# Talking-heads attention and squared-ReLU FFN on one core: when v and w_in are loaded in the first batch, and where dummy matmuls may stand

## The chip, the core and the metric

The kernel runs on one core of a Trainium2 chip. The metric is the device time of the whole program in microseconds (us). TensorE is called PE, VectorE DVE, ScalarE ACT, GpSimd POOL and SyncE SP, as in the profile.

## What is computed

The reference, cut to what matters (B = 8 batches, H = 12 heads, S = 448 tokens, D = 64; the FFN has 768 x 2048 and 2048 x 768 weights):

```python
scores = q @ k.T / 8                           # per batch and head
scores = einsum('bhij,hg->bgij', scores, w_pre)   # mix heads
attn   = softmax(scores)                          # over keys j
attn   = einsum('bhij,hg->bgij', attn, w_post)    # mix heads again
x      = (attn @ v)  -> (B*S, H*D) = (3584, 768)
out    = relu(x @ w_in)**2 @ w_out
```

## The kernel before, in words

**The stages of a batch.** q and k are transposed on PE (`t_qk`, L522; the last 64 tokens of q by `t_tail`, L550) and evacuated by DVE or ACT (L426, L428). `score` (L660) multiplies q and k for 128 query rows at a time, a row block `r` of which there are 3 and one of 64 rows (r = 0); the scores of all heads land, heads in the free dimension, in an `snat` tile. Mixing heads on PE needs the heads in the partition dimension, so SP issues DMAs within the on-chip memory that lay 10 tokens x 12 heads on 120 partitions (`relayout`, `move`, L689). There are 45 such chunks to a batch. In the first two row blocks of batch 0, three chunks share one larger move of 315 KB (a "triple") into five buffers, which are borrowed from tiles that are free then (`osb0`, `osb1`, and three in an `h2` tile, which the trace shows as `h`). In batch 0 the 18 triple chunks are mixed by three matmuls each (L780), all others by one (L784).

**A chunk** (`chunk`) is: mixing on PE (L780 or L784), maximum on DVE (L789), exp with its sum on ACT (L792), reciprocal on DVE (L798), the weights `wq` on POOL (L801), the second mixing on PE (L808), and its evacuation into `atb` by DVE or ACT. There are six sets of `es`, `mn`, `sm`, `rc`, `wq` (NE = 6): chunk n cannot be mixed before the second mixing of chunk n - 6 is through.

**After chunks.** `av` (L848) multiplies with v, ACT puts the result into `xt`, and FFN units follow as columns of tokens are complete: 96 matmuls with w_in (L901) per unit and row group, ReLU on ACT, square on POOL (L917), then matmuls with w_out (L933), evacuation and store.

**What sets the order.** Nothing is issued in the order in which it is written. Each operation is put into a `Planner` with an engine, an assumed duration in ns, a priority (chunk number plus an offset) and what it depends on; `run` goes through an assumed time and always takes the ready operation of the lowest priority on each engine. What comes out is one fixed order for each engine; on the chip every engine works through its list in that order and waits by semaphores. Score and relayout priorities contain the constant `AHEAD` (relayout: chunk number - AHEAD). Transfers are modelled as rows times ns, `alone` or `shared` with the other queue. Where PE has nothing ready, `run` may put in a dummy matmul on a zero tile (`still`, L1144), under the condition that the planner's model of PE's clock is slow or the share of busy time lately is under 0.55.

**Loads in the first batch.** POOL issues all loads: three of k, two of the q tails, three of q, ahead of everything else. `first_batch` then adds a POOL copy `hold` (L1067) that reads the `snat` tile of the r = 0 scores after it is complete; the two halves of v (336 KB each, `vs`) and after them the six tiles of w_in (512 KB each, `w1`, L1019) wait for this copy (`opened`). w_out follows in four loads that are gated by the `wq` of chunks 18, 21, 24, 27 (`gate`), and the q and k of batch 1 by those of chunks 13 and 16.

The dummy rule and the priority of a relayout read:

```python
if item is None and eng == "PE" and free and IDLE_FROM <= t < IDLE_END and (
    clock.at(t) > 1 or clock.share(t - SPELL, t) < IDLE_LOW
):
...
pri = n - AHEAD
```

Of the kernel before, what the change touches and what calls it, by code (L numbers as in the profile page):

```python
# [10 lines left out]
BF16 = mybir.dt.bfloat16  # L11
F32 = mybir.dt.float32

B, H, S, D = 8, 12, 448, 64
DMODEL = H * D
DFF = 2048
NPAIR = H // 2
# [22 lines left out]
PIECE = NPAIR // 2  # L40
NE = 6
NSCH = 11
AHEAD = 7.4
FIFO = 50
IDLE_NS, IDLE_COLS, IDLE_FROM, IDLE_END, IDLE_LOW = 112, 256, 1300, 130000, 0.55
SPELL, PHASE, DROP, RISE = 3413, 1700, 0.4, 0.8
# [29 lines left out]
TRI_IN = (0, 1)  # L76
W2_AT = [18, 21, 24, 27]
Q1_AT = [13, 16]
LAST_W1 = 4
TAIL0, Q0 = 19, 0.7  # L80
EARLY0 = 0

# [35 lines left out]
class Planner:  # L118
# [8 lines left out]
    def add(self, eng, ns, pri, fn, deps=(), lat=60, bank=None, frees=None, mode=0):  # L127
        op = Op(eng if isinstance(eng, dict) else {eng: ns}, lat, pri, fn, list(deps), bank, frees, mode)
        self.ops.append(op)
        return op  # L130
# [6 lines left out]
    def run(self):  # L137
        order, events, n = [], [], 0
# [21 lines left out]
        t, mode, clock = 0, 0, Clock()  # L160
# [16 lines left out]
        while True:  # L177
            for eng, heap in ready.items():
                if eng in queues:
                    x = queues[eng]  # L180
# [49 lines left out]
                        kept.remove(first)  # L230
                        item, op, args = first, first[2], []
                if item is None and eng == "PE" and free and IDLE_FROM <= t < IDLE_END and (
                    clock.at(t) > 1 or clock.share(t - SPELL, t) < IDLE_LOW
                ):
                    op = Op({"PE": 0}, 0, 0, self.still, [], None, None, mode)
                    op.eng, op.ns, op.at = "PE", IDLE_NS * clock.at(t), t
                    clock.spells.append((t, t + op.ns))
                    order.append((op, [free[0], mode]))
                    busy[eng] = t + op.ns
                    heapq.heappush(events, (t + op.ns, n, None))  # L240
                    n += 1
# [22 lines left out]
            t = events[0][0]  # L264
            while events and events[0][0] == t:
# [3 lines left out]
                if isinstance(op, tuple) and isinstance(op[0], Queue):  # L269
                    x, turn_ = op  # L270
# [29 lines left out]
def kernel(  # L300
# [11 lines left out]
    nc = tc.nc  # L312
    P = nc.NUM_PARTITIONS

    sb = ctx.enter_context(tc.tile_pool(name="sb", bufs=1))
# [9 lines left out]
    vs = sb.tile([P_KEYS, H, NB, D], BF16, name="vs")  # L325
# [32 lines left out]
    def load_kv(dst, src, b, h0, h1):  # L358
        nc.gpsimd.dma_start(
            out=dst[:, h0:h1, :, :].rearrange("p h r d -> p h (r d)"),  # L360
            in_=src[b, h0:h1].rearrange("h (p r) d -> p h (r d)", r=NB),
        )
# [5 lines left out]
    for what in LOADS0:  # L368
# [15 lines left out]
        out=smask[:, :], in_=ident[0:KC, 0:KC].rearrange("p (s h) -> p s h", s=CI), axis=AX.X, op=ALU.add,  # L384
    )
    wmix = many(3, "wmix", [KC, P], BF16)
    for t_ in wmix:
# [4 lines left out]
        out=nmask[:, :], in0=smask[:, :], scalar1=-SCALE, scalar2=1.0, op0=ALU.mult, op1=ALU.mult,  # L392
# [3 lines left out]
        out=perm[:, :].rearrange("k (s x p) -> k s x p", s=CI, x=2),  # L396
        in_=ident[0:KC, 0:KC].rearrange("k (s p x) -> k s x p", s=CI, x=2),
    )
    for t_ in wmix[1:]:
        nc.vector.tensor_tensor(  # L400
            out=t_[:, 0:KC].rearrange("p (s h) -> p s h", s=CI),
# [4 lines left out]
        out=wback[:, :, :], in0=wpost_rep[:, :].unsqueeze(2).to_broadcast([KC, H, CI]),  # L406
# [5 lines left out]
        out=keep_m[:, :], in_=ident[0:KC, 0:KC].rearrange("p (s m g) -> p m s g", s=CI, m=3), axis=AX.XY, op=ALU.add,  # L412
# [19 lines left out]
    add = pl.add  # L432
# [12 lines left out]
    def load(rows, each, pri, fn, deps):  # L445
        if len(loads) >= 7:
            deps = list(deps) + [loads[-7]]
        op = add("POOL", 750, pri, fn, deps, lat=850)
        done = pl.moved("LOAD", rows, each[0], each[1], 0, [op], 1500)
        loads.append(done)  # L450
        return done

    q_in, k_in, v_in = {}, {}, {}
# [43 lines left out]
    score_ops, scopy = {}, {}  # L497
# [45 lines left out]
    def t_tail(b, g):  # L543
        key = ("f" if b == 0 else "g", "z", b, g)
        old = [score_ops[b - 1, 0, p] for p in range(3 * g, 3 * g + 3)] if b > 0 else []

        def mms(slot):
            v_ = slot[:, :].bitcast(BF16)
            for i in range(3):
                nc.tensor.transpose(v_[:, i * P:(i + 1) * P], qt[:, 3 * g + i, :], ident[:, :])  # L550

        def put(eng):
            copy(
                eng, zt[:, 3 * g:3 * g + 3, :].rearrange("p a c -> p (a c)"),
                slots[key][:, :].bitcast(BF16)[:, 0:3 * P],
            )

        pri = b * NCHUNK - (19 if b > 0 else TAIL0) + 3 * g
        mm = add("PE", 200, pri, keep(key, mms), [tail_in[b]] + old, lat=200, bank=key)
        ev = add({"DVE": 360, "ACT": 440}, 0, pri, put, [mm], frees=key)  # L560
        got_tail.setdefault(b, []).append(mm)
        for p in range(3 * g, 3 * g + 3):
            ready_tail[b, p] = ev
# [63 lines left out]
    def flip(b, r):  # L627
        return 1 - r if b == 0 and r < 2 and EARLY == 0 else r
# [4 lines left out]
    def store_of(b, r):  # L633
        return snat[flip(b, r) % 2]
# [9 lines left out]
    def groups(b, r):  # L644
        size = GROUP if b >= GROUP_AT and r > 0 else 1
        return [range(p, p + size) for p in range(0, NPAIR, size)]

    def score(b, r, group):
# [13 lines left out]
        first = [0, EARLY, C0[2], C0[3]][r] if b == 0 else C0[r]  # L662
        pri = b * NCHUNK + first - AHEAD - 0.6 - (0.7 if r == 0 else 1.4) * (NPAIR - p)
        n = b * (NJ + 1) + r - 2
# [19 lines left out]
    def block_of(c):  # L684
        r = sum(c >= c0 for c0 in C0) - 1
        return r, c - C0[r]

    def move(n, pri, ns, deps, outs, srcs, lat):
        op = add("SP", ns, pri, lambda: nc.sync.dma_start(out=outs, in_=srcs), deps, lat=680)  # L689
        rows, alone, shared = (8, 160, 130) if ns == 800 else (12, 70, 38) if ns > 700 else (6, 70, 38)  # L690
        done = pl.moved("DMA", rows, alone, shared, 0, [op], 500)
        relay.setdefault(n, []).append(done)
        return done

    def relayout(b, c):
# [6 lines left out]
        deps = list(scopy[b, r]) + (list(scopy[b, r - 1]) if r == 1 and cc == 0 else [])  # L702
        pri = n - AHEAD
        if r == 2 and cc == 0:
# [279 lines left out]
    def gate(step):  # L984
        return [wq_op[step]] if step in wq_op else []
# [14 lines left out]
    started = add("POOL", int(1000 * at_) + 700, -100, lambda: None)  # L1000
# [17 lines left out]
    def load_w1(c2, pri, more=()):  # L1018
        w1_in.append(load(16, (152, 148), pri, lambda: nc.gpsimd.dma_start(  # L1019
            out=w1[c2][:, :], in_=moe_w_in[c2 * 128:(c2 + 1) * 128, 0:DFF], max_dma_last_dim=4096,  # L1020
        ), [started, *more]))
# [7 lines left out]
        done.next.append(w2_in[f4])  # L1029
        w2_in[f4].left += 1  # L1030

    def load_half(b, n, x, deps):
        h0 = x * H // 2
        v_in[b].append(load(42, (46, 58), n, lambda: load_kv(vs, v, b, h0, h0 + H // 2), deps))

    def load_v(b, n, deps):
        v_in[b] = [load(42, (46, 58), n, lambda h0=h0: load_kv(vs, v, b, h0, h0 + H // 2), deps) for h0 in (0, H // 2)]

# [14 lines left out]
    def first_batch():  # L1053
        for i in range(NPAIR):
            if i == 0:
                v_in[0] = []
                for x in range(0):
                    load_half(0, -30 + x, x, [started])
        for p in range(NPAIR):
            t_qk(0, p)  # L1060
        for g in range(2):
            t_tail(0, g)
        for r in (1, 0):
            for p in groups(0, r):
                score(0, r, p)
        hold = sb.tile([P, NPAIR], BF16, name="hold")
        opened = add("POOL", 150, -6, lambda: nc.gpsimd.tensor_copy(  # L1067
            out=hold[:, :], in_=store_of(0, 0)[:, 0:NPAIR, 0],
        ), scopy[0, 0])
        for x in range(0, 2):  # L1070
            load_half(0, -5 + 0.1 * x, x, [opened])
        for i in range(NPAIR):
            load_w1(i, -4 + 0.1 * i, [opened])
        for n, c in enumerate(ORDER0):
            if c in C0[2:]:
                for p in groups(0, block_of(c)[0]):
                    score(0, block_of(c)[0], p)
            relayout(0, c)
            chunk(0, c)
            if n in W2_AT:  # L1080
                load_w2(W2_AT.index(n), n)
            if n in Q1_AT:
                load_ahead(1, n, 6 * Q1_AT.index(n))
            if c == C0[1]:
                for g in range(3):
                    av(0, 0, g, 0, P_ROWS)
                unit(0, 0)
            if c == C0[2]:
                for g in range(3):
                    av(0, 0, g, P_ROWS, XA)  # L1090
            if c == C0[3]:
                for g in range(3):
                    av(0, 1, g, 0, P_ROWS)
                unit(0, 1)
        for g in range(3):
            av(0, 1, g, P_ROWS, XB)
        unit(0, 2)
# [87 lines left out]
```

## Time and profile before

| What | us |
|---|---|
| median of 3 runs (587.54, 588.30, 588.59) | 588.3 |
| the profiled execution: device time | 587.99 |
| the profiled execution: span of its instructions | 586.2 |
| PE busy in the span | 569.0 (97%) |
| DVE busy | 486.9 (83%) |
| ACT busy | 470.5 (80%) |
| POOL busy | 326.4 (56%) |

How to read it: the span runs from the first to the last instruction that the profiler recorded, so 1.8 us of the device time lie around it. PE's matmuls are pipelined and their ends are modelled, so "busy" is not the same as "at its peak"; the 51 dummies count as busy too. A wait is put down to the semaphore that came last. On ACT and DVE, which evacuate what PE makes and carry the softmax, idle time matters only while PE waits for them.

### The profile page before, as it was taken

How to read it: one execution, taken by the hardware profiler on the slowest of the kernel's cores; microseconds unless marked ns; L12 is line 12 of the kernel's file. 1: busy time of each engine (PE TensorE's matmuls, PEld its weight loads, DVE VectorE, ACT ScalarE, POOL GpSimd, SP SyncE). 2: the span in 40 equal slices, each digit the busy share in tenths (PEclk: the TensorE clock that was granted, in tenths of full speed). 3: DMA queues.
4: the chain of work that ended last, by engine and by line, in shares of the span. 5: the costliest groups of instructions: out<-in, count | busy, mean ns of one | idle time of the engine just before them, and what ended most of it. 6: DMA issues, size and time to landing. Idle time of an engine off the chain costs nothing.

```text
span 586.2 us, 17120 instructions
## 1 busy us (share of the span) xinstructions
PE 569.0 (97%) x5802; PEld 407.8 (70%) x5802; DVE 486.9 (83%) x1241; ACT 470.5 (80%) x1239; POOL 326.4 (56%) x600
## 2 busy tenths in 40 slices
PE   8798999999999999999999999999999999999996
PEld 5446866777668676767767776876767766868783
DVE  5698999998899999999898888989798898989201
ACT  4597998889888898988888878888889888788330
POOL 4537557546666538744865538744856633735340
PEclk9899999999999999999999999999999999999999
DMA  8999969964796449965797639954597547322021
GB/s 96 190 216 221 208 143 174 192 160 116 130 196 164 122 115 173 190 134 142 114 173 171 135 100 173 184 146 124 100 176 177 133 112 146 102 82 79 1 55 54
DMA packets 132086, 82.33 MB, mean 140 GB/s; under 512 B 59582, under 2 KB 126286, under 8 KB 131998
## 3 DMA queue, kind: packets, MB, share of 16 engines
q1 hardware_dynamic: 85214, 58.42, 41.1%
q0 software_dynamic: 46784, 22.81, 30.9%
q8 instruction: 45, 0.74, 0.6%
q14 instruction: 43, 0.35, 0.2%
HBM read 45.62 MB, written 11.01 MB: 97 GB/s over the span
## 4 chain that ended last, share of the span: by engine, by line
PE 85%; ACT 4%; DMA 3%; DVE 3%; POOL 2%; issue 2%; SPq 0%; DVEq 0%; POOLq 0%; ACTq 0%
PE bank L933 24%; PE bank L901 24%; PE bank L808 13%; PE bank L784 10%; PE bank L848 6%; PE bank L660 6%; ACT es L792 2%; DMA sch<-snat 1%; DVE mn L789 1%; DMA osb<-snat 1%; PE bank L780 1%; ACT snat L428 1%; ACT hr L914 1%; PE bank L522 1%; DMA qt<-in_q_dram 1%
## 5 line engine op out<-in xcount | busy, mean ns | idle before, releaser
L792 ACT ACTIVATE es<-bank,mn 120x448 bf16<-120x448 f32 x360 | 229.6, 644 | 39.2 <-DVE mn L789 34.1
L801 POOL TENSOR_SCALAR wq<-wback,rc 120x120 bf16<-120x120 f32 x360 | 130.6, 367 | 179.1 <-DVE rc L798 104.0
L789 DVE TENSOR_REDUCE mn<-bank 120x1 f32<-120x448 f32 x360 | 210.2, 612 | 7.7 <-PE bank L780 4.5
L933 PE MATMUL bank<-w,h 128*128 128x384 bf16 x896 | 174.3, 325 | 0.9 <-ACT es L792 0.5
L426 DVE CAST atb<-bank 112x480 bf16<-112x480 f32 (+3 forms) x227 | 142.5, 636 | 28.9 <-PE bank L808 26.2
L901 PE MATMUL bank<-xt,w 128*128 128x256 bf16 (+1 forms) x1632 | 164.5, 253 | 0.2
L901 PEld LDWEIGHTS <-w 128*128 128x128 bf16 x1632 | 135.7, 98 | 21.9 <-issue 2.3
L917 POOL TENSOR_TENSOR h<-hr 128x512 bf16<-128x512 f32 x112 | 116.3, 1039 | 54.2 <-ACT hr L914 51.9
L808 PEld LDWEIGHTS <-es 120*112 120x112 bf16 (+1 forms) x1440 | 116.7, 130 | 38.2 <-issue 7.6
L808 PE MATMUL bank<-wq,es 120*112 120x120 bf16 (+1 forms) x1440 | 129.1, 217 | 3.0 <-POOL wq L801 2.0
L933 PEld LDWEIGHTS <-h 128*128 128x128 bf16 x896 | 83.5, 97 | 54.9 <-issue 5.2
L784 PE MATMUL bank<-sch,wmix 120*128 120x448 bf16 x334 | 103.2, 353 | 0.3
L426 DVE CAST snat<-bank 128x448 bf16<-128x448 f32 x164 | 96.3, 614 | 4.8 <-PE bank L660 3.3
L428 ACT CAST atb<-bank 112x480 bf16<-112x480 f32 (+3 forms) x157 | 82.5, 541 | 16.3 <-PE bank L808 14.7
L914 ACT ACTIVATE hr<-bank 128x512 f32<-128x512 f32 x112 | 67.1, 599 | 30.9 <-PE bank L901 25.2
L428 ACT CAST snat<-bank 128x448 bf16<-128x448 f32 x172 | 84.9, 551 | 3.7 <-PE bank L660 2.9
L792 ACT ACTIVATION_READ_ACCUMULATOR es<-bank,mn 120x1 f32 x360 | 76.0, 211 | 0.0
L798 DVE RECIPROCAL rc<-sm 120x1 f32<-120x1 f32 x360 | 53.4, 155 | 14.2 <-ACT es L792 12.0
L948 DVE COPY osb<-bank 128x384 f32<-128x384 f32 x56 | 30.9, 551 | 31.6 <-PE bank L933 31.3
L660 PE MATMUL bank<-kt,qz 64*128 64x448 bf16 x288 | 42.5, 354 | 0.4 <-ACT atb L428 0.2
L784 PEld LDWEIGHTS <-wmix 120*128 120x128 bf16 x342 | 30.3, 98 | 16.6 <-issue 6.7
L848 PE MATMUL bank<-atb,vs 112*64 112x192 bf16 (+3 forms) x864 | 41.0, 250 | 0.4 <-ACT atb L428 0.4
(60 smaller groups left out, 261.8 us busy)
## 6 DMA issues: line engine op xcount, KB each, us to landing
sch<-snat SPq DMA_DIRECT2D x318, 105.0 KB
out_dram<-osb SPq DMA_DIRECT2D x23, 360.0 KB
vs<-in_v_dram POOLq DMA_DIRECT2D x16, 336.0 KB, 9.0
ks<-in_k_dram POOLq DMA_DIRECT2D x14, 336.0 KB, 9.9
qs<-in_q_dram POOLq DMA_DIRECT2D x14, 288.0 KB, 8.9
w<-in_moe_w_in_dram POOLq DMA_DIRECT2D x6, 512.0 KB, 20.9
w<-in_moe_w_out_dram POOLq DMA_DIRECT2D x4, 768.0 KB, 25.1
out_dram<-osb SPq DMA_DIRECT2D x8, 192.0 KB
```

The costliest lines, as they stand in the source:

```text
L426: nc.vector.tensor_copy(out=out_, in_=in_)
L428: nc.scalar.copy(out=out_, in_=in_)
L660: nc.tensor.matmul(slot[:, 0:S], lhsT=lhsT, rhs=kt[i][half, :, at_, :], start=True, stop=True)
L784: nc.tensor.matmul(slot[:, 0:S], lhsT=wm[0:rows, :], rhs=src[0:rows, :], start=True, stop=True,)
L789: nc.vector.tensor_reduce(out=mn[i][0:rows, :], in_=slots[mk][0:rows, 0:S], axis=AX.X, op=ALU.min)
L792: nc.scalar.activation(out=es[i][0:rows, 0:S], in_=slots[mk][0:rows, 0:S], func=ACT.Exp, scale=-1.0, bias=mn[i][0:rows, 0:1], accum_out=sm ...
L801: nc.gpsimd.tensor_scalar(out=wq[i][0:rows, :, 0:ns], in0=wback[0:rows, :, 0:ns], scalar1=rc[i][0:rows, 0:1], scalar2=1.0, op0=ALU.mult, o ...
L808: nc.tensor.matmul(slot[0:P_KEYS, jb * H * ns:(jb + 1) * H * ns], lhsT=es[i][0:rows, jb * P_KEYS:(jb + 1) * P_KEYS], rhs=wq[i][0:rows, :, ...
L848: nc.tensor.matmul(v_[64 * hh:64 * hh + 64, i, 0:x1 - x0], lhsT=vs[:, 2 * c2 + hh, jb, :], rhs=atb[half][:, jb, 2 * c2 + hh, x0:x1], start ...
L901: nc.tensor.matmul(slot[:, j * w:(j + 1) * w], lhsT=w1[c2][:, (f0 + j) * 128:(f0 + j + 1) * 128], rhs=xt[:, c2, a:z], start=(c2 == 0), sto ...
L917: nc.gpsimd.tensor_tensor(out=h2_[:, f0:f0 + nf, 0:w], in0=hr[gi % 2][:, :].rearrange("p (f c) -> p f c", f=nf), in1=hr[gi % 2][:, :].rear ...
L933: nc.tensor.matmul(slot[:, 0:384], lhsT=h2_[:, ft, mt * 128:(mt + 1) * 128], rhs=w2[:, ft, nt * 384:(nt + 1) * 384], start=(ft == 0), stop ...
```

## The change

v is loaded directly behind q, without the `hold` copy, which goes away. The six loads of w_in are gated by the `wq` of chunk 0 and have the priority 0. Three constants of the planner change: `AHEAD` 7.4 to 7.2, the assumed time per row of a triple move on an otherwise idle queue 160 to 205 ns, and a dummy is allowed in any PE gap of the planner's first 9000 ns.

```diff
-AHEAD = 7.4
+AHEAD = 7.2
...
-LAST_W1 = 4
+W1_AT = [0, 0, 0, 0, 0, 0]
...
                 if item is None and eng == "PE" and free and IDLE_FROM <= t < IDLE_END and (
-                    clock.at(t) > 1 or clock.share(t - SPELL, t) < IDLE_LOW
+                    t < 9000 or clock.at(t) > 1 or clock.share(t - SPELL, t) < IDLE_LOW
                 ):
...
-        rows, alone, shared = (8, 160, 130) if ns == 800 else (12, 70, 38) if ns > 700 else (6, 70, 38)
+        rows, alone, shared = (8, 205, 130) if ns == 800 else (12, 70, 38) if ns > 700 else (6, 70, 38)
...
-    def load_half(b, n, x, deps):
-        h0 = x * H // 2
-        v_in[b].append(load(42, (46, 58), n, lambda: load_kv(vs, v, b, h0, h0 + H // 2), deps))
...
             if i == 0:
-                v_in[0] = []
-                for x in range(0):
-                    load_half(0, -30 + x, x, [started])
+                load_v(0, -30, [started])
...
-        hold = sb.tile([P, NPAIR], BF16, name="hold")
-        opened = add("POOL", 150, -6, lambda: nc.gpsimd.tensor_copy(
-            out=hold[:, :], in_=store_of(0, 0)[:, 0:NPAIR, 0],
-        ), scopy[0, 0])
-        for x in range(0, 2):
-            load_half(0, -5 + 0.1 * x, x, [opened])
-        for i in range(NPAIR):
-            load_w1(i, -4 + 0.1 * i, [opened])
...
             chunk(0, c)
+            for i, at in enumerate(W1_AT):
+                if n == at:
+                    load_w1(i, n, gate(n))
```

In the order that results, POOL's list after the first loads is: `wback`, a memset, two loads of v, `wq` of chunks 0 and 1, six loads of w_in, `wq` of chunk 2 (before: `hold`, two of v, six of w_in, `wq` of chunks 0, 1, 2). PE's list has the same matmuls in all but the dummies: 79 in place of 51. They stand at: 22 ahead of the first transposes (18 before); 3 behind these, 1 behind the q tails and 4 behind the first three matmuls of L472 (none before); 11 ahead of the first mixing (16); 12 behind the mixing of chunk 7 (none); 9 in two groups until the first `av` (12 in five); and 17 in three groups around the 26th to 31st of the single-matmul chunks (5 in two). On SP the fourth triple of row block 1 stands ahead of the larger part of an `sch` move behind which it stood. The rest of the lists differs from before in the interleaving of chunks, scores and FFN matmuls over the whole kernel.

## The prediction

> **What bounds the kernel now.** I read the page first, its 40 slices of 14.7 us.
>
> ```profile
> span 586.2 us, 17120 instructions
> PE   8798999999999999999999999999999999999996
> ...
> PEclk9899999999999999999999999999999999999999
> ```
>
> PE is at nine tenths or more nearly everywhere; only the first five slices and the last show losses, and the clock dips in the second. From about 110 us on PE waits for almost nothing (the waits of PE behind 110 us add up to 1.1 us). So the time is PE's work plus what PE loses ahead of 110 us plus a tail, and every us by which the first batch reaches the same state earlier should come off the end. What does PE wait for? Its waits, in us in all, times, longest:
>
> ```profile
> PE bank L780 <- DMA osb<-snat: 3.0, 2, 2.8
> PE bank L808 <- POOL wq L801: 2.0, 5, 0.7
> PE bank L550 <- DMA qt<-in_q_dram: 1.4, 1, 1.4
> ```
>
> The largest is a relayout, the second triple of the scores. The timeline (start, us, engine, line, operation) shows it with what runs beside it:
>
> ```profile
> 14.86 1.83 SPq L689 DMA_DIRECT2D osb<-snat  x2
> ...
> 15.40 1.59 POOL L359 DMA_DIRECT2D vs<-in_v_dram  x2 [0.30 <-issue]
> ...
> 16.98 4.33 POOL L1019 DMA_DIRECT2D w<-in_moe_w_in_dram  x6
> ...
> 18.94 1.86 PE L780 MATMUL bank<-osb,wtri_all 120*128 120x448 bf16 x9 [0.25 <-DMA osb<-snat]
> ...
> 21.73 0.71 POOL L801 TENSOR_SCALAR wq<-wback,rc 120x120 bf16<-120x120 f32 x2 [0.43 <-DVE rc L798]
> ...
> 23.59 2.10 PE L780 MATMUL bank<-osb,wtri_all 120*128 120x448 bf16 x6 [2.79 <-DMA osb<-snat]
> ...
> 25.40 0.36 POOL L801 TENSOR_SCALAR wq<-wback,rc 120x120 bf16<-120x120 f32 x1 [2.96 <-DVE rc L798]
> ```
>
> The first triple is issued at 14.86 and is there at 18.94 (4.1 us); the second is issued at 15.8 and there at 23.59 (7.7 us, the chain of work has it as 7.74 us of DMA). Between them stand the v and w_in transfers, 0.67 and 3.07 MB, in the other queue. PE idles 2.79 us. The windows of 1 us (length, PE busy, granted clock, DMA share, GB/s) show two more things:
>
> ```profile
> 13.00:14.00 1.00, 1.00 (x12) 1.00 0.00 0
> ...
> 22.00:23.00 1.00, 0.00 (x0) 1.00 1.28 184
> 23.00:24.00 1.00, 0.41 (x3) 0.98 1.16 208
> 24.00:25.00 1.00, 1.00 (x4) 0.50 1.21 306
> 25.00:26.00 1.00, 1.00 (x7) 0.50 1.11 286
> 26.00:27.00 1.00, 1.00 (x4) 0.50 1.12 277
> 27.00:28.00 1.00, 1.00 (x9) 0.81 1.15 260
> ```
>
> The gap costs twice: the granted clock is 0.50 from about 23.98 to 27.39 us (0.02 + 3 x 0.50 + 0.19 = 1.71 us of full-speed work lost). And the DMA engines move almost nothing from 12 to 16 us, when v could have been moved.
>
> **The change part by part.**
>
> *v behind q.* POOL is free of its loads and its two set-up instructions at 8.3 us and then stands still until `hold` at 14.91. Two issues (1.59 us) end at 9.9. q's transfers end by about 11.7 us (92 GB/s in the window 11:12, 16 in the next). In the windows from 4 to 11 us the loads moved 150 to 196 GB/s; 0.67 MB at 170 take 4.0 us, so v ends near 15.7, where it began to move before. It overlaps the first triple for a us or so; bounds 0 to +1 us on that, hidden in part by the next item.
>
> *The second triple's wait.* Without v and w_in beside it, it follows the first. In the windows from 16 to 19 us 142, 169 and 58 GB/s were moved, 0.37 MB, about the first triple's 315 KB: 2 us for one, 0.9 us of issue for the lower bound. So it is there 0.9 to 2.0 us behind the first, while PE mixes the first triple's chunks (9 matmuls, 1.86 us). The wait falls from 2.79 to 0 to 0.2: **-2.7 us**. With it falls the half clock, since PE was busy 0.63 of 3.4 us ahead of it and would now have the second triple's 2.0 us at full clock in that stretch: **-1.7 us** (the chain runs through PE from 23.59 to 27.6, so it counts in full; lower bound 0, if the idle time comes back, see the second rival). Next late are the maxima and exps: DVE and ACT are busy 2.0 of 5 us from 19 to 24 and 6.00 of 6 from 30 to 36, so the early chunks use idle time there.
>
> *Eight more dummies ahead of 9 us.* 18 dummies took 4.02 us, 223 ns each, and 16 later took 1.92, 120 ns: PE starts at half speed, though the clock column reads 1.00 there. It was still slow at 11.78 (two score matmuls in 0.93 us; 0.68 at 13.42). Four more ahead of the first transposes let these begin at 5.97 in place of 5.34; they take 0.96, and the next operation waits for the q tail until 7.68, so this and the three dummies behind are covered (cover about 0.7 us; without it +0.7). The other five (1 and 4) are in front of ready work: 0.6 us at full, 1.1 at half speed. Against it, PE is then busy from 1.06 to 8 us with no gap over 0.1 us, where it sat idle 1.38 us before 7.68. At 27.39 full speed came back after 3.8 us of busy PE and at 23.98 it went after 82% of idleness in 3.4 us, so I take full speed by 8 us at the latest. PE is busy 6.0 of 6 us from 9 to 15 us, of which 4.5 us at half speed; at most 2.2 us can be had. But DVE and ACT are busy 4.8 and 4.5 of these 6 us and the loads of q land at 10.2, 11.1 and 12.3 (issue plus 4.7 to 5.2), so I take a little more than half, 1.4, less 0.6: **-0.8 us**, bounds -1.6 and +1.1.
>
> The Trainium skill ("TensorE: Matmul & The Clock Gate", Part 1) says that the clock's window is free-running and does not start with the kernel. The trace cannot show this in one execution. By that rule the kernel before is at full speed early in some of its runs, this term is 0 on the whole, and the sum would be -2.8 us.
>
> *w_in behind two `wq`.* Nothing waits for w_in soon: its issues end at 21.3 before, the last lands near 46, its first matmul is at 54.2. But the six issues now stand in front of the `wq` of chunk 2. With the first chunk some 0.8 us earlier, `wq` 1 ends near 21.5, the issues take 4.33 us, and `wq` 2 comes at 25.8; before at 25.40. Six chunks' buffers (NE) let chunks 2 to 7 be mixed and exponentiated meanwhile; chunk 8 needs the second mixing of chunk 2. Then `wq` 2 to 7 follow at 0.36 us each and end at 28; before, `wq` 7 came at 33.2. So the block costs nothing against before, but it holds ACT and DVE from about 25.6 (eight exps at 0.83 from 19) to 27.5: 2 us, in which only score copies of the next row block can run. I take **+1.1 us**, bounds 0 and +4.3 (the whole issue on the path). The 12 dummies there (1.4 us) stand in that wait: 0, bound +1.4.
> Transfers: the queue that brings w_in starts 4.5 us later but without v ahead (0.67 MB, 4 us) and with five triples already gone, so it is done by 46 again at the latest, against a first use near 50.6.
>
> *12 more dummies near 84 us* (17 for 5): 12 x 0.12 = 1.4 us if nothing is waited for, 0 if PE idles there anyway, which it did (window 84:90: 4.67 of 6 us busy, five dummies among it). **+0.4**.
>
> *AHEAD and 205 ns* change the interleaving everywhere. A fifth of a chunk, with 45 chunks in about 73 us per batch, is 0.3 us of later relayouts. No PE wait for a relayout is listed behind 110 us, so something covers it, but not how much is shown. **+0.1**, bounds -0.5 and +1.5.
>
> **The sum:** -2.7 - 1.7 - 0.8 + 1.1 + 0.4 + 0.1 = **-3.6 us**; 587.99 - 3.6 = **584.4 us**. The profiled execution is 0.3 us under the median of its runs. The count of finished chunks says the same: `wq` 7 is 5.2 us earlier, but of the work of DVE and ACT before 33.2 six score copies of 0.6 us are left to do, 3.6 us on two engines, 1.8 us: 3.4 us ahead.
>
> **The rivals.**
> 1. *Gained and given back* (587.3, between 586.4 and 588.6). Behind 30 us DVE and ACT are the pace (6.00 of 6 us each from 30 to 36), and from 19 to 72 us the DMA engines are at a share of 0.9 to 1.4. The early chunks arrive, but relayouts and the w_out loads do not come earlier: the chain of work shows 8.2 us of DMA for an `sch` at 57.16. v moved early is 4 us of transfer saved; w_in started later loses about 1 MB at most where a relayout runs alone. If about 3 us of the 3.6 come back as PE gaps between 60 and 95 us, where the planner itself puts 17 dummies, 0.7 are left. For: those numbers. Against: PE had w_in units to fill with, 5.6 to 6.0 of 6 us busy in 54 to 84. The Trainium skill ("DMA: Bandwidth & Descriptors", Queues, rings and completion order) says that each engine takes turns between the queues packet by packet; 7.7 against 4.1 us for two equal triples agrees. By it relayouts during w_in stay slow wherever w_in is put, so the loss only moves.
> 2. *Slower: the wait moves to POOL* (589.6, between 588.6 and 591). If chunks 2 to 7 are not ahead when the six issues begin, PE has next to nothing between `wq` 1 and `wq` 2, idles 4.3 us again and gets half clock again. Then -2.7 and -1.7 are lost, and the dummies' 0.6 (head), 0.5 (near 84) and the 0.5 of the rearranged order stand: 588.0 + 1.6. It decides from PE busy under about 0.2 to 0.4 of the 3.4 us ahead of `wq` 2 (0.18 lost the clock before). Against: the planner's order has chunks 5, 6 and 7 in front of it.
> 3. *AHEAD uncovers relayouts in all batches:* 0.3 us in each of 28 later row blocks is 8 us, 592 with the gain. Against: no such wait now.
>
> **How the numbers follow.** Forecast (582 to 586.4) 0.55; rival 1 0.22; rival 2 0.19; rival 3 0.04. A measurement of this kernel tells about 0.2%, 1.2 us, from no change: faster is under 587.1, the forecast and half of rival 1's lower side, 0.64; same 0.14, the rest of rival 1 and a little of rival 2; slower 0.22. The range leaves out rival 3 and the outer ends of the others: 581.5 (the sum with the head at -1.6, the block and the dummies near 84 us at 0 and the last term at -0.5 is -6.5) to 589.7.
>
> **What would show it.** Right: no PE wait for `osb` over 0.5 us, no granted clock of 0.5 behind 10 us, second mixing triple at about 20 us, `wq` 7 near 28. Wrong in the head: first `osb` issue after 15 us. Wrong in the block: PE or ACT idle over 2 us ahead of `wq` 2. Given back: the same early gain, but the first w_out matmul (93.4 us before) not earlier by 3.

## The result and the profile after

The changed kernel takes 592.87 us (median of 6 runs, 592.14 to 595.39); the kernel before took 587.93 beside it (6 runs, 587.51 to 588.59). The ratio is 1.0081 [1.0061, 1.0101]: slower by 5 us (0.8%), clear of noise, where 584.4 was predicted. The profiled execution took 594.75 us with a span of 593.0, so it lies 1.9 us above the median of its runs, and it is 6.8 us above the execution that the prediction started from. The page of the kernel after answers to the first lines shown of before:

```profile
span 593.0 us, 17166 instructions
...
PE   7888999999999999999999999989999999999996
...
PEclk9899999999999999999999999999999999999999
```

The head looks much the same. What is new is a single 8 far behind, in slice 27 (385 to 400 us). The windows of both kernels (length; busy time of PE, PEld, DVE, ACT, POOL; clock; DMA share; GB/s) show where PE's time is lost. Before:

```profile
110.00:130.00 20.00, 20.00 (x246) 15.54 (x245) 19.33 (x54) 17.35 (x47) 9.51 (x21) 1.00 0.82 179
...
300.00:400.00 100.00, 99.67 (x1005) 71.96 (x1004) 88.51 (x227) 84.05 (x225) 55.96 (x105) 1.00 0.80 154
```

After:

```profile
110.00:130.00 20.00, 19.51 (x233) 13.91 (x232) 18.57 (x50) 17.70 (x48) 10.53 (x21) 1.00 0.79 174
...
300.00:400.00 100.00, 96.59 (x983) 70.18 (x981) 85.91 (x223) 84.03 (x223) 59.18 (x109) 1.00 0.82 149
```

PE is busy 3.1 us less between 300 and 400 us, where no load of the first batch is left.

Busy time alone can't say how far the work has come. So I count PE's matmuls by kind, each kind with a fixed weight (190 ns for a mixing matmul, 163 for one with w_out, and so on, from typical spacings in the trace), leave the dummies out, and ask when a given share of this work is through:

| Share of PE's work | before, us | after, us | after is behind by |
|---|---|---|---|
| 5% | 54.3 | 53.6 | -0.8 |
| 9% (near the end of the first batch's chunks) | 80.1 | 79.8 | -0.4 |
| 17% | 126.5 | 129.0 | +2.4 |
| 30% | 199.2 | 202.4 | +3.2 |
| 50% | 309.9 | 314.0 | +4.2 |
| 60% | 365.5 | 371.4 | +5.8 |
| 65% | 392.8 | 400.6 | +7.9 |
| 100% | 581.5 | 588.3 | +6.8 |

The changed first batch is through 0.4 us earlier. Everything else, 7.2 us, is lost behind it, in the last 86% of the span, where the diff moves no load.

**The first batch.** Timeline of the kernel after (start, us, engine, line, operation; in brackets the idle time before it and its releaser):

```profile
8.25 1.60 POOL L359 DMA_DIRECT2D vs<-in_v_dram  x2
...
14.20 1.83 SPq L689 DMA_DIRECT2D osb<-snat  x2
...
19.12 4.68 PE L780 MATMUL bank<-osb,wtri_all 120*128 120x448 bf16 x15 [1.59 <-DMA osb<-snat]
...
23.76 4.33 POOL L1019 DMA_DIRECT2D w<-in_moe_w_in_dram  x6
28.13 2.07 POOL L801 TENSOR_SCALAR wq<-wback,rc 120x120 bf16<-120x120 f32 x6
```

The second triple's wait is gone: fifteen mixing matmuls (both triples) run without a gap. But PE now waits 1.59 us for the first triple, which lands 4.9 us after its issue (4.1 before), and the fifteen take 4.68 us, which is half speed. The windows say so:

```profile
16.20:19.61 3.41, 1.82 (x16) 1.30 (x15) 1.46 (x3) 1.68 (x4) 0.00 (x0) 1.00 0.69 180
19.61:23.02 3.41, 3.41 (x11) 1.37 (x9) 2.00 (x5) 1.60 (x5) 0.00 (x0) 0.50 0.92 263
```

**Behind the first batch.** The waits of PE behind 85 us (us in all, times, longest), and one of ACT's:

```profile
PE bank L784 <- ACT snat L428: 2.0, 2, 1.5
PE bank L808 <- POOL wq L801: 1.7, 4, 1.1
...
ACT snat L428 <- DMA sch<-snat: 5.5, 3, 3.0
```

Before, ACT never waited there for an `sch` move that still read its `snat` tile. The largest of these, in order of time (SP, ACT, PE):

```profile
374.38 4.96 SPq L598 DMA_TRANSPOSE kt<-kn  x1
379.47 3.43 SPq L604 DMA_TRANSPOSE qz<-qn  x1
383.00 2.95 SPq L689 DMA_DIRECT2D sch<-snat  x3
...
389.04 2.42 SPq L689 DMA_DIRECT2D sch<-snat  x3
...
391.83 0.53 ACT L428 CAST snat<-bank 128x448 bf16<-128x448 f32 x1 [2.97 <-DMA sch<-snat]
...
392.41 0.35 PE L784 MATMUL bank<-sch,wmix 120*128 120x448 bf16 x1 [1.49 <-ACT snat L428]
```

In the kernel before, the same stretch of SP's list:

```profile
377.51 1.42 SPq L598 DMA_TRANSPOSE kt<-kn  x1
379.03 1.61 SPq L604 DMA_TRANSPOSE qz<-qn  x1
380.73 6.82 SPq L689 DMA_DIRECT2D sch<-snat  x8
```

Here the two transposes for the next batch hold SP for 8.4 us in place of 3.0; the relayouts queued behind them come late; ACT's next instruction is a score copy into a tile that such a relayout has yet to read; the exps queued behind it on ACT wait too, and PE runs dry.

### The profile page after: what moved, and what is told of

The parts are those of the page before. It is cut to its first block, busy times and chain, and to the rows that moved or that the text cites. A ratio compares the mean times of both kernels' runs of the same rounds, so it can differ in the third digit from the quotient of the medians.

```text
span 593.0 us, 17166 instructions
## 1 busy us (share of the span) xinstructions
PE 570.5 (96%) x5830; PEld 407.9 (69%) x5830; DVE 482.9 (81%) x1236; ACT 475.8 (80%) x1247; POOL 325.0 (55%) x596
## 4 chain that ended last, share of the span: by engine, by line
PE 80%; DVE 6%; ACT 5%; issue 3%; DMA 3%; POOL 2%; DVEq 0%; ACTq 0%; POOLq 0%
PE bank L933 24%; PE bank L901 21%; PE bank L808 12%; PE bank L784 10%; PE bank L848 6%; PE bank L660 5%; ACT es L792 2%; DVE mn L789 2%; DVE atb L426 2%; DMA sch<-snat 2%; DVE snat L426 1%; POOL h L917 1%; DMA osb<-snat 1%; ACT snat L428 1%; PE bank L780 1%
## 5 line engine op out<-in xcount | busy, mean ns | idle before, releaser
L426 DVE CAST atb<-bank 112x480 bf16<-112x480 f32 (+3 forms) x222 | 136.8, 628 | 27.8 <-PE bank L808 25.9
L808 PE MATMUL bank<-wq,es 120*112 120x120 bf16 (+1 forms) x1440 | 127.4, 217 | 7.8 <-POOL wq L801 4.5
L426 DVE CAST snat<-bank 128x448 bf16<-128x448 f32 x161 | 94.6, 614 | 6.5 <-PE bank L660 2.7
L428 ACT CAST atb<-bank 112x480 bf16<-112x480 f32 (+3 forms) x162 | 85.9, 546 | 14.4 <-PE bank L808 13.4
L428 ACT CAST snat<-bank 128x448 bf16<-128x448 f32 x175 | 86.4, 552 | 8.0 <-DMA sch<-snat 5.5
L660 PE MATMUL bank<-kt,qz 64*128 64x448 bf16 x288 | 41.3, 354 | 0.1
```

Source lines behind the costliest of these rows:

```text
L426: nc.vector.tensor_copy(out=out_, in_=in_)
L428: nc.scalar.copy(out=out_, in_=in_)
L660: nc.tensor.matmul(slot[:, 0:S], lhsT=lhsT, rhs=kt[i][half, :, at_, :], start=True, stop=True)
L808: nc.tensor.matmul(slot[0:P_KEYS, jb * H * ns:(jb + 1) * H * ns], lhsT=es[i][0:rows, jb * P_KEYS:(jb + 1) * P_KEYS], rhs=wq[i][0:rows, :, ...
```

## The experiments

Three theories. **A:** the smaller `AHEAD` issues relayouts too late in all batches (rival 3's mechanism). **B:** the first batch is what costs: early v, the POOL block, or the dummies. **C:** neither value nor load costs; any change makes the planner write another order for the whole kernel, and the order before happens to have few stalls. No kernel below leaves out any of the computation; only dummies are removed or added.

Beside each kernel ran the kernel before; times are medians, ratios are to it, with the 95% interval.

### One part at a time, planned anew

Edits: e1 is the kernel after with `AHEAD` put back, e2 the kernel before with the new `AHEAD`, e3 the kernel before with v alone behind q, e4 with w_in alone behind the `wq` of chunk 0.

```diff
e1, in the kernel after:    -AHEAD = 7.2   +AHEAD = 7.4
e2, in the kernel before:   -AHEAD = 7.4   +AHEAD = 7.2
e3: -                for x in range(0):
    +                for x in range(2):
    ...
    -        for x in range(0, 2):
    +        for x in range(2, 2):
e4: -        for i in range(NPAIR):
    -            load_w1(i, -4 + 0.1 * i, [opened])
    ...
    +            if n == 0:
    +                for i in range(NPAIR):
    +                    load_w1(i, n, gate(n))
```

> The changed kernel with AHEAD back at 7.4; everything else of the change stays (v behind q, w_in behind the first wq, dummies ahead of 9 us, 205 ns). Theory A, relayouts and scores that come a fifth of a chunk later cost the later batches: the lag that grew from about 90 to 400 us (from 0.7 to 7.9 us in PE work) goes, 587 to 588.5 us, and ACT waits for sch<-snat (5.5 us behind 85 us in the changed kernel) go to about 0. Theory B, what the first batch hands over is worse: AHEAD does not matter, 592 to 594. Theory C, every new order of the planner scatters by some us with no single cause: anything from 585 to 595, and not the sum of its parts with the next run.

> The kernel before with AHEAD 7.2 alone. Theory A: 591.5 to 593.5 us, level with before until about 90 us, then a lag that grows, with ACT waiting for sch<-snat by several us. Theory B: 587.5 to 588.5. Theory C: off by some us in either direction, not matching what the run with AHEAD 7.4 in the changed kernel gains.

> The kernel before with v alone loaded behind q; w_in stays behind the hold copy. Theory A: within 1 us of before, 587 to 589, since the second triple still shares the DMA engines with w_in: it lands about 7 us after its issue. Theory B: a part of the loss, 589 to 591. My own prediction's term for v (0 to +1 us on the first triple) would show in the first triple landing up to 1 us later after its issue than 4.1 us.

> The kernel before with the six w_in loads alone moved behind the wq of chunk 0; v stays behind the hold copy. By the prediction's terms the second triple's wait (-2.7) and perhaps the half clock (-1.7) go and POOL's block (+1.1) comes: 584 to 586. Theory A: the early gain is given back by chunk 8 as in the changed kernel, so 587 to 589. Theory B: 590 to 593.

| Kernel | us | ratio |
|---|---|---|
| e1: after, `AHEAD` 7.4 | 598.09 | 1.0173 [1.0117, 1.0228] |
| e2: before, `AHEAD` 7.2 | 601.55 | 1.0226 [1.0189, 1.0264] |
| e3: before, v early | 597.24 | 1.0137 [1.0106, 1.0168] |
| e4: before, w_in later | 592.03 | 1.0059 [1.0034, 1.0084] |

A falls: the same step from 7.4 to 7.2 costs 2.3% in the kernel before and in the changed kernel saves 0.9% (1.0173 to 1.0081). A cause with a price of its own would keep its sign. Of the three parts tried alone, two cost more than all together (2.3 and 1.4% against 0.8%) and the third 0.6%; prices that simply add up would need a large gain from the rest, the 205 ns and the dummies ahead of 9 us, which were not tried alone. The next runs had to part the order from the loads.

### The order kept, only loads moved; and a change without meaning

In e5, e6 and e7 the planner of the kernel before writes its list, and only then are the loads moved in it: v behind q, w_in behind the `wq` of chunk 1, or both. (`load_ops` holds the two loads of v and then the six of w_in.) The lists of PE, DVE, ACT and SP stay as they were, dummies included; `hold` stays too, but a load that is moved no longer waits for it. e8 changes `AHEAD` in the kernel before by a thousandth, which means nothing on the chip but breaks ties in the planner.

```diff
-        for op, args in pl.run():
+        seq = pl.run()
+        early = [x for x in seq if x[0] in load_ops[0:2]]        # v: e5, e6
+        seq = early + [x for x in seq if x[0] not in load_ops[0:2]]
+        late = [x for x in seq if x[0] in load_ops[2:8]]         # w_in: e5, e7
+        seq = [x for x in seq if x[0] not in load_ops[2:8]]
+        at = 1 + max(i for i, x in enumerate(seq) if x[0] in (wq_op[0], wq_op[1]))
+        seq[at:at] = late
+        for op, args in seq:
...
e8: -AHEAD = 7.4   +AHEAD = 7.401
```

> The order that the planner makes of the kernel before, kept on every engine, with the change's loads put into POOL's list by hand: v behind q, w_in behind the wq of chunk 1. AHEAD, the dummies and the 205 ns stay as before. Theory C, the four runs so far are slow because each is a new order, and the loads as such are harmless or good: 584 to 588 us. Theory B, the loads themselves hurt what follows: 590 to 595. By my prediction's terms for these two edits (-2.7, -1.7, +1.1) 585.

> The order of before with v alone put behind q in POOL's list. Theory C: 587 to 589.5 (the planned variant of the same edit took 597.2 beside 589.1 of before). Theory B: 595 to 598, like the planned variant.

> The order of before with the six w_in loads alone put behind the wq of chunk 1 in POOL's list; v stays behind the hold copy. Theory C: 585 to 589. Theory B: 591 to 593, like the planned variant.

> The kernel before with AHEAD 7.401 for 7.400: a thousandth of a chunk, 2 ns of a chunk's time, has no meaning on the chip, but breaks ties between priorities, so that most of the order of PE, DVE and ACT is another. Theory C: off from before by 3 to 12 us, most likely slower. Theories A and B: 588 to 590, as before.

| Kernel | us | ratio |
|---|---|---|
| e5: order before, v and w_in moved | 587.59 | 0.9973 [0.9949, 0.9998] |
| e6: order before, v moved | 591.35 | 1.0034 [1.0014, 1.0054] |
| e7: order before, w_in moved | 589.65 | 0.9996 [0.9978, 1.0013] |
| e8: before, `AHEAD` 7.401 | 592.97 | 1.0052 [1.0018, 1.0086] |

The loads as the change puts them gain 0.3% if the order stays. The same edits planned anew cost 1.4% (e3 against 0.3% of e6) and 0.6% (e4 against 0 of e7). And a thousandth of `AHEAD` costs 0.5%. This is what C says of the order. That a mere draw of the order explains all of the 2.3% of e2 isn't shown: no change without meaning, here or below, cost more than 0.8% beside its own starting point.

e5 also shows what the loads do by themselves. Its timeline:

```profile
18.87 3.00 PE L780 MATMUL bank<-osb,wtri_all 120*128 120x448 bf16 x15
...
22.32 4.33 POOL L1019 DMA_DIRECT2D w<-in_moe_w_in_dram  x6
26.70 1.04 POOL L801 TENSOR_SCALAR wq<-wback,rc 120x120 bf16<-120x120 f32 x3
...
27.12 0.37 PE L808 MATMUL bank<-wq,es 120*112 120x120 bf16 x4 [3.34 <-POOL wq L801]
```

Both triples are mixed at full speed without a wait, and then PE waits 3.34 us for the `wq` of chunk 2 behind the six w_in issues and has half the clock from about 27.4 to 30.8. This is rival 2's mechanism. From 9% of the work to the end, e5 stays 1.1 to 1.3 us ahead of before: with the order kept, a lead of the first batch does come off the end, as the prediction took it. e6 shows why v alone gains nothing and loses 0.3%: w_in still runs beside the second triple, for which PE waits 5.2 us. In e7 v does, and PE waits 3.2 us.

### Less of the POOL block; the other half of the cross; a second change without meaning

e11 is e5 with w_in issued in pairs behind the `wq` of chunks 1, 2 and 3; e12 is e11 with 4 more dummies at the start and 3 ahead of the q tails. e9 is the reverse of e5: the order after on every engine, dummies included, but with `hold`, v and w_in ahead of the first `wq` as in the kernel before. e10 changes a constant of the planner's model by 1 ns. (`held` are the eight loads, `picked` their entries in the list, which are taken out first.)

```diff
e11: +        wq_firsts = [(wq_op[0], wq_op[1]), (wq_op[2],), (wq_op[3],)]
     +        for n in range(3):
     +            at = 1 + max(i for i, x in enumerate(seq) if x[0] in wq_firsts[n])
     +            seq[at:at] = [picked[op] for op in held[2 + 2 * n:4 + 2 * n]]
e12: +        dummies(4, pe[0])
     +        dummies(3, pe[tails[0]])
e9:  +        at = 1 + max(i for i, x in enumerate(seq) if x[0] in scopy[0, 0])
     +        seq[at:at] = [(add("POOL", 150, 0, hold_copy), [])] + [picked[op] for op in held]
e10: -SLACK = {"PE": 200, "SP": 800, "POOL": 100}
     +SLACK = {"PE": 201, "SP": 800, "POOL": 100}
```

> The order that the planner makes of the changed kernel, kept on every engine, with the loads of before put into POOL's list by hand: a hold copy, v and w_in behind it, ahead of the first wq. AHEAD 7.2, 205 ns and the 28 extra dummies stay. Theory C, the order of the later batches costs the time and the loads are worth 1 to 2 us: 592 to 596, with the lag behind 90 us as in the changed kernel (6 to 7 us of PE work from there to the end). Theory B, the loads cost it: 587 to 589.

> The kernel before with one planner constant off by a nanosecond (SLACK of PE 201 for 200): a second order without a meaning on the chip, different in about half of PE's rows. Theory C: not the time of before; 588 to 598, more likely 591 to 595. If it is within 1 us of before, the scatter of orders is smaller than the first such run made it look, and the cause is more in what the edits do.

> The order of before; v behind q, and the w_in loads in pairs behind the wq of chunks 1, 2 and 3, so that POOL is held 1.5 us at a time and not 4.33. In the graft with all six together PE waited 3.34 us for wq 2 and got half clock from 27.6 to 31.0. If that wait is what took the gain there: 584 to 586 beside about 588.5 of before, no wait over 1 us of PE between 19 and 30 us and no half clock there. If the early chunks are bound by ACT and DVE anyway: 587 to 588, as with six together.

> As the run with w_in in pairs, with four more dummies ahead of the first transposes and three between them and the q tails, all else in the order of before. My prediction's term for the head says that PE comes to full speed by 8 us and the first triple is issued up to 1.4 us earlier: 0.5 to 1.4 us under the run with pairs. If the head is bound by loads and evacuation, or if the clock's phase differs from run to run: no difference.

| Kernel | us | ratio |
|---|---|---|
| e9: order after, loads as before | 595.11 | 1.0095 [1.0065, 1.0125] |
| e10: before, `SLACK` 201 | 590.14 | 1.0015 [0.9995, 1.0034] |
| e11: order before, v early, w_in in pairs | 587.35 | 0.9972 [0.9953, 0.9990] |
| e12: e11 with 7 more dummies | 587.92 | 0.9974 [0.9956, 0.9992] |

e9 closes the cross: the order after is slow with the old places of the loads too, and its transposes at the place shown above are long as well:

```profile
375.67 4.81 SPq L598 DMA_TRANSPOSE kt<-kn  x1
380.61 2.34 SPq L604 DMA_TRANSPOSE qz<-qn  x1
```

The pairs were to give back what the POOL block takes, but they only divide the wait: in e11's profiled execution PE waits 0.48, 0.88 and 1.45 us for the `wq` of chunks 2, 3 and 4, 2.8 us in all against 3.34 in e5, and still has half the clock, from 27.8 to 34.6 us. e11 isn't told apart from e5, nor e12 from e11, although e12's profiled execution reaches its sixth exp 1.6 us before e11's (24.27 against 25.85 us). e5, e11 and e12 beat both kernels, by 0.3% against before.

### Changes without meaning around the kernel after, and its late dummies

e13 and e14 do to the kernel after what e8 and e10 did to before. e15 is the order after without the last 17 dummies. e16 takes a thousandth of `AHEAD` the other way in the kernel before.

```diff
e13: -AHEAD = 7.2   +AHEAD = 7.201
e14: -SLACK = {"PE": 200, ...   +SLACK = {"PE": 201, ...
e15: +        idle_ = [i for i, x in enumerate(seq) if x[0].fn is pl.still]
     +        drop = set(idle_[-17:])
e16: -AHEAD = 7.4   +AHEAD = 7.399
```

> The changed kernel with AHEAD 7.201 for 7.200, which has no meaning on the chip but gives another order. If the changed kernel's loss behind 90 us is a draw: off from its 592.9 by 2 us or more in either direction, 588 to 600. If it belongs to AHEAD near 7.2 and the loads: 592 to 594.

> The changed kernel with SLACK of PE 201 for 200. Draw: 588 to 600 and not the same as the run with 7.201. Edit: 592 to 594.

> The order of the changed kernel without the last 17 dummies, those near 84 us; nothing else moves. If they take time from work that is ready: up to 2 us faster than the changed kernel, 591 to 592 (my prediction had 0.4 for 12 of them). If they stand where PE waits for the softmax anyway: 592.5 to 593.5, with as much idle time in their place.

> The kernel before with AHEAD 7.399. If the order of before is a lucky draw, 590 to 598, as with 7.401 (0.5% slower). If orders near it are as good, 588 to 590.

| Kernel | us | ratio |
|---|---|---|
| e13: after, `AHEAD` 7.201 | 593.57 | 1.0080 [1.0055, 1.0104] |
| e14: after, `SLACK` 201 | 597.69 | 1.0160 [1.0116, 1.0203] |
| e15: after without 17 dummies | 590.89 | 1.0043 [1.0008, 1.0078] |
| e16: before, `AHEAD` 7.399 | 591.21 | 1.0045 [1.0022, 1.0068] |

Five changes without meaning move the time by 0.15 to 0.5% around before, and by 0 and 0.8% around after; all come out slower or the same. Two of them, e10 and e13, can't be told apart from their starting points, and by the marks set for them ahead of the run that speaks against C. But they are small draws: PE's list in e10 is that of before up to 259 us, in e13 that of after up to 118 us; in e8 it parts from before at 37 us, in e16 at 100 us. So the size of a draw can't be told from five. The first batch of e14 is the same as after's (PE's list up to 162 us), and behind it another stall is the worst: not on SP, but on DVE, whose list has a copy of the next batch's k ahead of its arrival (DVE, then PE):

```profile
431.21 0.29 DVE L585 COPY kn<-ks 112x512 bf16<-112x512 bf16 x1 [3.86 <-DMA ks<-in_k_dram]
431.42 1.15 DVE L426 CAST snat<-bank 128x448 bf16<-128x448 f32 x2
...
432.09 0.42 PE L808 MATMUL bank<-wq,es 120*112 120x120 bf16 x4 [2.65 <-DVE snat L426]
```

Without the 17 dummies, PE isn't faster through the place where they stood (26.2 us from 9% to 13% of the work, 25.6 in after): it idles and the clock falls. Windows of e15, columns as above:

```profile
78.00:84.00 6.00, 3.67 (x41) 2.33 (x39) 4.86 (x14) 5.42 (x15) 3.45 (x6) 1.00 0.53 124
84.00:90.00 6.00, 5.77 (x77) 3.59 (x77) 4.24 (x12) 5.50 (x17) 2.29 (x6) 0.72 0.38 130
```

Nine of e15's ten runs spread from 588.99 to 597.31 us, and its interval overlaps that of after; so the dummies may cost the 2 us between the medians or nothing; the stretch in which they stand doesn't show a cost.

### All orders by one measure

Time from 9% to 92% of PE's work, counted as above, and PE's idle time in it:

| Order | us | PE idle, us |
|---|---|---|
| before (before, e5; with e6, e7, e11, e12: 459.5 to 460.1) | 459.7, 459.8 | 3.0, 3.1 |
| near before (e10, e8, e16) | 462.6, 463.6, 464.3 | 4.2, 5.2, 6.7 |
| one part, planned anew (e4, e3, e2) | 465.2, 465.7, 473.5 | 6.1, 5.5, 10.4 |
| after (e9, e15, after) | 464.7, 465.7, 466.8 | 5.6, 6.3, 7.0 |
| near after (e13, e14, e1) | 466.0, 471.6, 472.7 | 5.5, 8.5, 9.8 |

These are single executions, and the three in the row of after, which have one order but for e15's dummies, differ by 2 us. But the six with the order before agree to 0.6, and every other order is at least 2.5 us above them. The time rises with the idle time and by more than it. A part of the rest is the clock: in e15, e8, e1 and e2 it falls to half once more in this stretch, at 84, 89, 371 and 437 us, for 3.41 us each time, 1.7 us of full-speed work.

## Why the prediction was wrong

**The step that failed** is the last term of the sum, "AHEAD and 205 ns change the interleaving everywhere", +0.1 us with bounds -0.5 and +1.5. In its place the stretch behind the first batch measured +7.1 us in the profiled execution (466.8 - 459.7), +5.0 in the same order with the loads as before (e9). Of the 7.1, 4.0 are more PE idle time; 12 more dummies near 84 us, which had a term of their own, account for about 1.5 (2.35 us of PE busy for the 17, 0.88 for the 5); the remaining 1.6 I can't assign. The price was set by a mechanism, a relayout 0.3 us later, and by its cover now. What changed was every engine's list, and the loads alone change it too (e3, e4), which their terms left out. The question should have been how much another list of the same kind costs. The prediction had the material for a bound on one side: PE idles 3 us in 460 there, so another order could gain little more than that and could lose much. It read "no such wait now" as a property of the work. It is one of that order.

**Rival 3** gave the time (592), but by luck: a smaller lead of the relayouts is not what costs, since e1, with the old `AHEAD`, is slower still. What it lacked was new waits of any other kind in a new order, against which "no such wait now" is no argument.

**The second triple's wait** (-2.7): right. It is gone in after and in e5, not in e6 and e7, where one of the two loads still runs beside it.

**Its half clock** (-1.7): not settled by the change, but from execution to execution. In after and e13 the clock falls behind the new wait for the first triple (1.59 and 2.00 us); in e14 and e15, whose first batch has the same order, it doesn't, behind 0.63 and 0.83 us. The executions part at v: its second half lands 8.9 and 8.7 us after its issue in after and e13, 7.3 and 7.5 in e14 and e15, and the first triple 4.9 and 5.3 us after its issue against 4.0 and 4.2. Why v lands late in some executions isn't known. The lines of e14:

```profile
17.86 3.00 PE L780 MATMUL bank<-osb,wtri_all 120*128 120x448 bf16 x15 [0.63 <-DMA osb<-snat]
...
26.13 0.70 PE L808 MATMUL bank<-wq,es 120*112 120x120 bf16 x8 [0.99 <-POOL wq L801]
```

**The head** (-0.8): right in size and in kind. The first triple is issued 0.66 us earlier in after (14.20) and 0.97 to 1.20 in e13, e14 and e15. PE is at full speed by about 6 us: the 16 first transposes take 0.62 us, before 0.96. The alternative, that this term is 0 because before has full speed early in some of its runs, doesn't hold in e6 and e11, which have before's head: the granted clock is full from 5.0 and 3.9 us, but falls again 3.41 us later, and the first triple is issued at 15.07 and 15.09. *v's overlap*, though: in after the first triple lands 4.9 us after its issue and not 4.1, while v is there until 18.0 and not 15.7. The bound of +1 us was right; taking none of it was not.

**The POOL block** (+1.1): `wq` 2 to 7 begin at 28.13 in after and 25.67 in e14 (25.8 forecast), end at 30.2 and 27.7 (28 forecast), and PE waits 0.83 and 0.99 us for them. The lead over before shrinks from the 6th to the 9th exp by 2.2 us in after (-2.3 to -0.1) and by 2.2 in e14 (-4.9 to -2.7): about twice the forecast, within its bounds. Rival 2's mechanism shows in full only in e5, where fewer chunks' mixing and no dummies stand ahead of `wq` 2.

**The dummies near 84 us** (+0.4): e15 allows 0 to 2 us.

**The first batch in all** was to bring 4.1 us (the sum without its last two terms, which lie behind it). At 9% of the work, e14 and e15 are 2.9 us ahead of before, after and e13 0.4; they part at v's landing, the wait for the first triple and the clock behind it. So the terms of the first batch were sound in kind and too large, and 7 us behind it swallowed them. The mark "first w_out matmul not earlier by 3" misleads: it is 3.9 us earlier (89.53), but the new order has it earlier among the others, behind 856 matmuls that are no dummies in place of 948.

**What stays open:** why the order before has so few stalls. The traces show what each stall hangs on (a transpose on SP, a copy whose load isn't there, a `wq`), not what would foresee it; and no experiment here let the planner work with corrected durations.

## What to carry to other kernels

Where a planner writes a fixed order and PE is at 99%, price an edit in two parts: what it does in place, and a new draw of the whole order. Here every kernel planned anew came out slower than before, by up to 2.3%, or the same (e10). Measure the second part with several changes that mean nothing, and part the two by moving the edited instructions within the old list. Here the gain, which was smaller than most draws, was had only with the order kept (e5, e11, e12).

## What the runs showed of the hardware

The clock falls more easily than the prediction had it: in after it went after a window of 3.41 us in which PE was busy for 1.82 us, 53%, its longest gap 1.59 us (the windows above). In e15, whose 3.41 us stretches lie at the same places, the same window was busy for 2.59 us, 76%, and the clock stayed. But in e7 it fell at 47.7 us behind a window that was 72% busy, with no gap over 0.69 us, so the share at which it falls is not settled. The half-speed stretches are 3.41 us or 6.83, twice that, but where the grid lies differs between executions of the same first batch: the first entry in the record of the granted clock is at 5.98 us in after, 6.48 in e13 and 4.19 in e14. That agrees with the Trainium skill ("TensorE: Matmul & The Clock Gate", Part 1), which calls the window free-running. The same section puts the fall after an idle window; here PE was busy for over half of it, and the measurement decides.

A `DMA_TRANSPOSE` of the same shape on SP (L598) took from 1.37 us to 4.96 us in the kernel after, median 1.71, and what follows it in SP's list stands behind it. The order seems to set which one is long: with the order of after it is the ninth of twelve (4.96, 4.81 in e9, 5.12 in e15), with the order of before the third (3.83, 4.39 in e5, 4.69 in e6), so before has a long one too. The v loads of after, which were forecast to be there at 15.7 us, landed at about 16 and 18, 7.7 and 8.9 us after their issue.
